# Other tables of order and places, searched on with GpSimd's column operations missing turns

## The chip, the cores and the metric

The kernel runs on one NeuronCore of a Trainium2 chip. The metric is the device time of one execution in microseconds (us), the median of several runs. The core has five engines that run side by side, each through its own queue in the order in which the program issued its work: TensorE (PE, matrix products, with PEld for its weight loads), VectorE (DVE), ScalarE (ACT), GpSimd (POOL) and SyncE (SP, which here only issues DMAs). An instruction that needs another engine's result waits for it, and what is queued behind it on its engine waits with it.

## The reference

The input is x, 2048 rows of 512 float32 values. A layer norm of x goes into two branches, which are multiplied:

```
xn = layernorm(x)
# A: linear attention, 32 heads of 16
q, k, v = split(xn @ wqkv)
pq, pk = phi(q), phi(k)                  # phi(t) = (t + 1 if t > 0 else exp(t)) + 1e-6
o = (pq @ (pk^T v)) / (pq . sum(pk) + 1e-6)
s = o @ wo
# B: a mixer over neighbouring rows, then an MLP
h = gelu(layernorm(xn) @ w1)             # its four quarters are shifted by +1, -1, +2, -2 rows
x1 = xn + shifted(h) @ w2
b = x1 + gelu(layernorm(x1) @ w3) @ w4   # w3: 512 x 1376
out = x + s * silu(b)
```

## The kernel before

The rows lie in 16 tiles of 128 rows, and four tiles make a block. A float32 matrix product is done as three products of rounded parts: each operand is split into a high part (a copy rounded on ScalarE, names that end in `h`) and a low part (what is left, a subtraction on VectorE, names that end in `l`). `products` (line names L133 for all matmuls) issues high x high, high x low and low x high. Many products are also folded by sums of quarters, for which VectorE makes the forms (`xf`, `kq_f`).

The program doesn't issue its work at once. `Plan.add` collects some 5,700 operations in the order of the source, each with its engine and what it reads and writes. They are 3,315 of TensorE, 860 of VectorE, 812 of ScalarE, 216 of GpSimd and 491 of SP. `Plan.emit` then issues them in the order of a written table, `ORDER_OF_ALL`, in which a number n stands for the n-th operation that was added. A second table, `PLACES`, holds the buffer number of each of 1,781 tiles in the pools. So the first table alone sets the order of each engine's queue, and both together set which buffer is reused and when.

GpSimd has three kinds of work. It issues the DMAs that add to what is in the buffer (`gather`, L212). It works on halo columns (two columns of a tile, L538 and L539). And it makes the statistics of the layer norms on columns, 128 partitions by one to four values: `scale_x` makes `w` (L183), `rs` by a power (L451), `ns` (L183) and `nm` (L178) for a block of rows. `spread` makes for a block the two rows of values that the branch B needs:

- `pu` and minus the mean (`an`) on GpSimd, then the power into `an` (L451),
- a transposition of `an` on TensorE into `ab` (L138), a copy to `ar` on ScalarE, and two stores by SP into the rows `arow` and `nrow` in memory,
- from `nrow` GpSimd's gathers add the row to the block's transposed input `xt`, whose parts `u_0h` to `u_3l` and forms `xs_0h` to `xs_3l` are the operands of the products of q and k in that block (`pbx`, `pex`, `pax`).

Blocks are numbered 0 to 3: `ab1` stands first in TensorE's queue, then `ab0`, `ab2` and `ab3`. The profile leaves out such numbers, so all four are `ab` there. `x4` to `x7` are the normalized tiles of block 1, made by ScalarE from `rs` and `nm`.

VectorE's operations are of two kinds for what follows: those with two inputs in SBUF (the subtractions of the low parts, the forms, most of `kr`, `ke` and `qr`) and those that read PSUM (`qi`, `qk`, `kt`) or one input (the `bn_stats` of block 1).

Of the kernel before, what the change touches and what calls it, by code (L numbers as in the profile page):

```python
# [245 lines left out]
def linear_attn_gated_by_mixer(  # L246
# [1336 lines left out]
    for b in LINE:  # L1583
# [11 lines left out]
        0, 15, 16, 4, 12, 20, 1, 11, 17, 2, 14, 23, 32, 18, 44, 19, 13, 53, 21, 22, 97, 35, 45, 26, 46, 98, 47, 174,  # L1595
        123, 48, 29, 24, 96, 33, 175, 25, 105, 49, 38, 102, 124, 99, 103, 51, 41, 34, 108, 106, 125, 100, 176, 54,
        104, 50, 101, 109, 56, 27, 126, 52, 62, 36, 55, 28, 107, 111, 37, 59, 112, 30, 113, 301, 243, 65, 178, 110,
        114, 31, 3, 115, 127, 177, 117, 179, 118, 6, 66, 5, 119, 240, 180, 142, 186, 158, 246, 116, 67, 39, 128,
        120, 42, 143, 68, 237, 181, 129, 203, 69, 204, 43, 121, 182, 159, 40, 205, 474, 187, 130, 160, 206, 207, 70,
        57, 9, 161, 122, 131, 71, 162, 163, 7, 183, 164, 58, 165, 483, 144, 135, 166, 63, 74, 145, 146, 244, 10, 75,  # L1600
        132, 147, 220, 167, 221, 60, 76, 8, 222, 197, 64, 188, 200, 77, 223, 260, 224, 133, 61, 225, 78, 189, 477,
        241, 136, 403, 83, 247, 148, 184, 194, 480, 84, 195, 242, 190, 191, 79, 256, 149, 137, 248, 198, 501, 245,
        85, 238, 226, 150, 80, 86, 284, 72, 285, 268, 168, 286, 134, 208, 239, 138, 192, 169, 209, 193, 88, 210,
        250, 139, 211, 151, 212, 249, 89, 199, 251, 196, 185, 227, 152, 287, 170, 272, 215, 201, 288, 140, 289, 153,
        87, 252, 290, 92, 402, 291, 253, 292, 309, 81, 255, 228, 404, 202, 232, 264, 154, 281, 293, 73, 481, 213,
        302, 278, 214, 155, 305, 275, 229, 296, 257, 279, 303, 294, 337, 93, 280, 156, 269, 331, 311, 230, 304, 273,
        261, 171, 231, 274, 90, 276, 313, 325, 265, 282, 172, 349, 338, 283, 141, 216, 475, 334, 335, 332, 94, 482,
        277, 366, 339, 336, 306, 484, 363, 367, 340, 307, 328, 317, 405, 326, 233, 333, 321, 360, 368, 364, 406,
        314, 365, 476, 407, 341, 369, 342, 322, 1133, 343, 258, 344, 408, 310, 295, 478, 345, 743, 329, 259, 727,
        330, 315, 361, 82, 362, 312, 217, 487, 346, 254, 347, 234, 297, 348, 95, 409, 262, 410, 497, 350, 411, 357,  # L1610
        319, 157, 358, 390, 327, 370, 354, 263, 412, 413, 266, 386, 373, 546, 414, 392, 91, 394, 355, 388, 356, 493,
        359, 393, 415, 416, 505, 395, 396, 417, 423, 267, 424, 270, 418, 419, 479, 316, 430, 420, 389, 425, 485,
        426, 397, 421, 431, 400, 391, 427, 486, 432, 271, 422, 433, 434, 488, 371, 401, 435, 547, 428, 436, 308,
        442, 443, 429, 444, 235, 548, 509, 445, 323, 387, 446, 236, 489, 218, 549, 510, 490, 550, 298, 551, 320,
        492, 447, 398, 553, 219, 318, 554, 555, 491, 437, 511, 556, 399, 733, 557, 173, 378, 558, 449, 438, 450,
        559, 451, 494, 448, 452, 374, 453, 454, 579, 498, 552, 455, 580, 581, 582, 379, 372, 583, 512, 560, 439,
        459, 324, 513, 460, 351, 461, 502, 567, 440, 456, 568, 462, 299, 382, 463, 506, 464, 614, 352, 300, 465,
        584, 615, 381, 380, 611, 441, 469, 561, 724, 562, 617, 526, 470, 563, 569, 620, 522, 457, 564, 565, 570,
        471, 525, 571, 621, 566, 353, 572, 472, 618, 385, 495, 619, 629, 458, 616, 573, 496, 626, 730, 612, 514,
        377, 627, 585, 635, 628, 574, 613, 531, 586, 499, 587, 575, 588, 751, 589, 593, 622, 500, 590, 375, 591,  # L1620
        535, 632, 466, 473, 636, 592, 637, 885, 542, 638, 639, 594, 630, 503, 596, 530, 597, 507, 598, 534, 599,
        576, 536, 631, 747, 600, 532, 538, 601, 577, 796, 540, 640, 703, 376, 623, 602, 624, 642, 533, 641, 625,
        537, 633, 603, 539, 634, 643, 656, 606, 541, 657, 644, 725, 649, 543, 700, 544, 658, 467, 659, 660, 726,
        661, 508, 2057, 645, 646, 662, 595, 504, 650, 709, 518, 701, 607, 647, 710, 383, 675, 578, 521, 676, 648,
        711, 468, 384, 677, 678, 608, 679, 545, 680, 728, 668, 681, 669, 706, 731, 651, 609, 652, 734, 704, 653,
        604, 654, 729, 685, 686, 737, 605, 687, 732, 670, 702, 707, 735, 671, 755, 688, 672, 655, 517, 673, 736,
        797, 674, 689, 738, 690, 705, 691, 803, 712, 804, 663, 759, 805, 739, 760, 708, 664, 740, 718, 519, 713,
        742, 798, 692, 799, 529, 761, 806, 800, 1121, 695, 693, 807, 741, 714, 808, 801, 694, 809, 719, 756, 715,
        1134, 716, 802, 717, 829, 748, 665, 830, 810, 515, 831, 666, 744, 832, 833, 523, 811, 516, 834, 752, 812,
        696, 817, 720, 721, 762, 697, 861, 864, 763, 862, 1135, 698, 813, 610, 764, 814, 863, 520, 873, 682, 722,  # L1630
        818, 887, 819, 820, 683, 821, 822, 723, 870, 823, 988, 871, 865, 772, 767, 872, 835, 867, 684, 868, 1136,
        768, 836, 785, 775, 837, 1153, 524, 874, 757, 1122, 815, 869, 784, 843, 838, 758, 839, 816, 840, 1175, 841,
        781, 866, 780, 824, 876, 1068, 667, 877, 842, 878, 788, 886, 882, 883, 786, 745, 1181, 879, 782, 880, 1154,
        776, 825, 846, 847, 848, 1157, 787, 849, 826, 779, 906, 789, 1158, 899, 1117, 790, 900, 827, 771, 881, 749,
        907, 1201, 875, 746, 884, 908, 783, 527, 909, 1129, 910, 750, 964, 853, 911, 791, 901, 794, 699, 850, 851,
        912, 902, 795, 903, 1159, 904, 792, 965, 844, 966, 1183, 852, 932, 854, 933, 905, 934, 1160, 935, 889, 855,
        936, 856, 888, 937, 845, 1118, 920, 890, 921, 922, 793, 895, 923, 924, 1163, 857, 753, 925, 970, 1184, 971,
        528, 926, 972, 1155, 1002, 896, 913, 891, 914, 967, 754, 858, 1003, 893, 939, 940, 897, 892, 941, 828, 1004,
        859, 915, 894, 1123, 916, 982, 1171, 942, 943, 944, 1141, 976, 1125, 977, 945, 1167, 973, 989, 974, 1143,
        975, 956, 1165, 985, 1067, 949, 777, 917, 918, 978, 968, 1005, 1124, 969, 1006, 986, 957, 1007, 919, 950,  # L1640
        951, 1144, 938, 958, 987, 927, 1009, 860, 1010, 1008, 952, 928, 2162, 953, 1011, 1069, 1012, 1168, 929,
        1023, 1104, 1161, 954, 765, 1016, 1130, 930, 898, 1017, 955, 1013, 778, 1014, 1088, 959, 1177, 1018, 1019,
        1015, 766, 1024, 1178, 1025, 983, 773, 992, 1156, 1020, 984, 960, 769, 1026, 1173, 1070, 1027, 774, 1089,
        961, 1035, 1162, 1036, 770, 1119, 1085, 1179, 979, 946, 962, 980, 981, 1166, 1073, 1021, 990, 1037, 1139,
        1038, 991, 1028, 1169, 1090, 993, 1029, 1039, 1126, 1074, 1086, 1087, 1071, 1097, 947, 1079, 1022, 1042,
        1137, 1120, 1040, 1043, 994, 1230, 1072, 1044, 998, 1045, 1041, 1140, 1298, 1046, 1075, 1047, 1142, 1103,
        1100, 1138, 1048, 1082, 1296, 1083, 1084, 1000, 999, 1101, 1030, 1052, 1053, 995, 1131, 1054, 1098, 1077,
        1094, 1132, 997, 1095, 1096, 2172, 996, 1055, 1076, 1151, 1080, 2056, 1059, 1081, 1078, 1091, 1170, 1049,
        1092, 1056, 1105, 1149, 1127, 1057, 1297, 1031, 1202, 1203, 1058, 1150, 1216, 1050, 1102, 1231, 1147, 1232,
        1107, 1304, 1051, 1217, 1152, 1106, 1204, 948, 1205, 1032, 1145, 1128, 1233, 1206, 1109, 1033, 1099, 1093,  # L1650
        2068, 1234, 1110, 1148, 1062, 1235, 1236, 1146, 1244, 1063, 1112, 1218, 1199, 1245, 1286, 1207, 2069, 1064,
        1219, 1176, 1299, 1305, 1220, 931, 1221, 2066, 1246, 1108, 1237, 1060, 1238, 1113, 1208, 1180, 1321, 1065,
        1306, 1239, 1115, 1174, 1209, 1240, 2059, 1189, 1247, 1114, 1248, 1210, 1172, 1241, 2058, 1116, 1249, 1200,
# [353 lines left out]
```

## Time and profile before

| | us |
|---|---|
| median of three runs | 506.41 (505.35 to 509.16) |
| the profiled execution | 505.57 |
| its span, from the first instruction to the last | 503.9 |
| mean granted TensorE clock over the span | 0.994 of full speed |

The times in the views are counted from the start of the span. A line of the order of time has the start, the duration, engine, source line, operation, what is written and read by the program's names without buffer numbers, the shapes, a count, and in brackets the idle time of the engine just before with what ended it. In the view of waits a line says who waited for whom, the sum in us, the number of waits and the longest.

### The profile page before, as it was taken

How to read it: one execution, taken by the hardware profiler on the slowest of the kernel's cores; microseconds unless marked ns; L12 is line 12 of the kernel's file. 1: busy time of each engine (PE TensorE's matmuls, PEld its weight loads, DVE VectorE, ACT ScalarE, POOL GpSimd, SP SyncE). 2: the span in 40 equal slices, each digit the busy share in tenths (PEclk: the TensorE clock that was granted, in tenths of full speed). 3: DMA queues.
4: the chain of work that ended last, by engine and by line, in shares of the span. 5: the costliest groups of instructions: out<-in, count | busy, mean ns of one | idle time of the engine just before them, and what ended most of it. 6: DMA issues, size and time to landing. Idle time of an engine off the chain costs nothing.

```text
span 503.9 us, 10127 instructions
## 1 busy us (share of the span) xinstructions
PE 491.9 (98%) x3340; PEld 449.4 (89%) x3340; DVE 436.4 (87%) x860; ACT 377.9 (75%) x871; POOL 142.9 (28%) x220
## 2 busy tenths in 40 slices
PE   9999799999999999999999999999999999999996
PEld 5777587888688989898999999999999999999996
DVE  5999696696999989899999999989989889886764
ACT  5999699795876888999899877566688746664531
POOL 1795802555643131331022000000000034443230
PEclk9999899999999999999999999999999999999999
DMA  7959696899898798989779878764779999999998
GB/s 240 317 124 281 132 301 197 177 327 281 219 285 222 181 262 226 234 223 270 245 182 269 289 245 282 229 221 144 211 229 308 300 237 212 277 245 282 271 245 234
DMA packets 90925, 121.60 MB, mean 241 GB/s; under 512 B 10744, under 2 KB 42392, under 8 KB 90872
## 3 DMA queue, kind: packets, MB, share of 16 engines
q1 hardware_dynamic: 78488, 98.93, 60.4%
q0 software_dynamic: 12384, 22.03, 26.1%
q8 instruction: 26, 0.43, 0.4%
q14 instruction: 27, 0.22, 0.1%
HBM read 74.63 MB, written 42.09 MB: 232 GB/s over the span
## 4 chain that ended last, share of the span: by engine, by line
PE 68%; DVE 2%; DMA 2%; ACT 1%; issue 1%; SPq 1%; DVEq 0%; ACTq 0%
PE pbd L133 12%; PE pb L133 11%; PE h L133 8%; PE ped L133 6%; PE pe L133 5%; PE pbs L133 4%; PE pad L133 3%; PE pbm L133 3%; PE pa L133 3%; PE a L133 2%; PE pes L133 2%; PE pem L133 2%; PE g L133 2%; PE pas L133 1%; DMA y_0t<-y_0d 1%; PE pam L133 1%
## 5 line engine op out<-in xcount | busy, mean ns | idle before, releaser
L212 POOL DMA_DIRECT2D xo<-x1d x12 | 10.9, 907 | 147.9 <-DVE xo L178 138.5
L212 POOL DMA_DIRECT2D o<-xnd x16 | 14.2, 908 | 67.2 <-ACT o L155 30.8
L155 ACT ACTIVATE th<-xo 128x512 f32<-128x512 f32 (+1 forms) x16 | 9.9, 617 | 17.5 <-DVE xo L188 9.6
L212 POOL DMA_DIRECT2D zacc<-ke x12 | 10.7, 891 | 38.9 <-DMA zacc<-ke 10.6
L212 POOL DMA_DIRECT2D th<-in_x x14 | 12.5, 945 | 29.8 <-DVE th L188 16.9
L212 POOL DMA_DIRECT2D xt<-nrow x16 | 15.2, 1245 | 1.3 <-DMA nrow<-ar 0.9
L183 POOL TENSOR_SCALAR w<-mv 128x4 f32<-128x4 f32 (+2 forms) x10 | 4.8, 478 | 37.5 <-ACT sq L155 37.2
L155 ACT ACTIVATE y<-o,nm,rs 128x512 f32<-128x512 f32 x16 | 12.3, 807 | 0.0
L155 ACT ACTIVATE ht<-ht 128x512 f32<-128x512 f32 x16 | 9.9, 624 | 2.5 <-DVE ht L178 2.5
L155 ACT ACTIVATE sq<-o,mv 128x512 f32<-128x512 f32 x16 | 11.5, 720 | 0.2
L155 ACT ACTIVATE u<-pb 128x256 f32<-128x256 f32 x20 | 7.6, 381 | 5.3 <-PE pb L133 5.2
L188 DVE SCALAR_TENSOR_TENSOR qz<-pq,zb 128x512 f32<-128x512 f32 x16 | 10.9, 681 | 0.8 <-ACT zb L155 0.6
L178 DVE TENSOR_TENSOR ht<-h,abc 128x512 f32<-128x512 f32 x16 | 10.9, 686 | 0.6 <-PE h L133 0.5
L188 DVE SCALAR_TENSOR_TENSOR pq<-pq,rd 128x512 f32<-128x512 f32 x16 | 10.8, 681 | 0.2
L1278 DVE TENSOR_REDUCE den<-qz 128x32 f32<-128x512 f32 x16 | 10.9, 679 | 0.1
L155 ACT ACTIVATE sq<-o 128x512 f32<-128x512 f32 x16 | 10.0, 628 | 0.6 <-DMA o<-xnd 0.3
L155 ACT ACTIVATE pa<-pb 128x256 f32<-128x256 f32 x20 | 7.3, 368 | 4.0 <-PE pb L133 3.8
L451 POOL TENSOR_TENSOR rs<-w,nhalf 128x4 f32<-128x4 f32 (+2 forms) x10 | 9.8, 982 | 0.8
L155 ACT ACTIVATE p<-pe 128x256 f32<-128x256 f32 x20 | 7.6, 378 | 2.7 <-PE pe L133 2.6
L155 ACT ACTIVATE x<-x,nm,rs 128x512 f32<-128x512 f32 x12 | 9.4, 804 | 0.0
L155 ACT ACTIVATE xo<-pbd 128x256 f32<-128x256 f32 x6 | 2.3, 382 | 9.0 <-PE pbd L133 9.0
L155 ACT ACTIVATE sq<-x,mv 128x512 f32<-128x512 f32 x12 | 8.5, 711 | 0.0
(2018 smaller groups left out, 2526.1 us busy)
## 6 DMA issues: line engine op xcount, KB each, us to landing
w_s<-in_w SPq DMA_DIRECT2D x23, 256.0 KB, 5.1
x<-in_x SPq DMA_DIRECT2D x16, 256.0 KB, 5.1
xt<-in_xt SPq DMA_DIRECT2D x16, 256.0 KB, 5.7
xnd<-x SPq DMA_DIRECT2D x16, 256.0 KB, 4.4
xt<-nrow POOLq DMA_DIRECT2D x16, 256.0 KB, 6.8
pqd<-qr SPq DMA_DIRECT2D x16, 256.0 KB, 3.6
pq<-pqd SPq DMA_DIRECT2D x16, 256.0 KB, 3.9
o<-xnd POOLq DMA_DIRECT2D x16, 256.0 KB, 5.5
```

Of the source, the lines that this page charges most:

```text
L133: lambda: nc.tensor.matmul(out.get(), lhs.get(), rhs.get(), start=start, stop=stop, skip_group_check=more))
L155: nc.scalar.activation(out.get(), src.get(), func, scale=get(scale), **kw)
L178: self.vec(eng, out, [a, b], lambda: self.e(eng).tensor_tensor(out.get(), a.get(), b.get(), op=op), True)
L183: lambda: self.e(eng).tensor_scalar(out.get(), a.get(), get(s1), get(s2), **kw), False,
L188: lambda: self.nc.vector.scalar_tensor_tensor(out.get(), a.get(), get(s), b.get(), op0=op0, op1=op1),
L212: lambda: self.nc.gpsimd.dma_start(out.get(), get(src), accum_op=ALU.add), mb=mb)
L451: lambda: g.tensor_tensor(out.get(), src.get(), nh.get(), op=ALU.pow))
L1278: pl.add("DVE", .6, .68, [t], [den], lambda: nc.vector.tensor_reduce(den.get(), t.get().rearrange("p (h d) -> p h d", d=DH), axis=AX.X, op ...
```

## The change

Both tables are replaced, and nothing else. Every operation, its operands' names, engine and arithmetic stay as they were. In the new tables 398 of the 3,315 TensorE operations have the same rank in TensorE's queue as before; the median shift is 3 ranks and the largest 45. VectorE's median shift is 1 rank (largest 29), ScalarE's 2 (42), GpSimd's 1 (39) and SP's 3 (29). 1,432 of the 1,781 buffer numbers differ. The description of the change says how the new tables were made: by searching on from tables like these with the rule that GpSimd's column operations miss their turns between VectorE's operations.

The diff is two tables of some 370 lines each way. This is its core, the first two lines of the order and the stretch with block 2's `pu` (number 486) and its power (488):

```diff
     ORDER_OF_ALL = (
-        0, 15, 16, 4, 12, 20, 1, 11, 17, 2, 14, 23, 32, 18, 44, 19, 13, 53, 21, 22, 97, 35, 45, 26, 46, 98, 47, 174,
-        123, 48, 29, 24, 96, 33, 175, 25, 105, 49, 38, 102, 124, 99, 103, 51, 41, 34, 108, 106, 125, 100, 176, 54,
...
-        426, 397, 421, 431, 400, 391, 427, 486, 432, 271, 422, 433, 434, 488, 371, 401, 435, 547, 428, 436, 308,
...
+        1, 16, 0, 20, 2, 5, 11, 15, 4, 12, 17, 13, 3, 23, 14, 32, 18, 45, 19, 35, 21, 44, 97, 22, 6, 26, 46, 174,
+        98, 47, 53, 123, 24, 48, 29, 33, 108, 175, 25, 96, 105, 34, 49, 38, 99, 124, 106, 109, 51, 41, 107, 50, 102,
...
+        388, 407, 357, 358, 91, 390, 414, 361, 312, 254, 394, 362, 368, 408, 392, 415, 497, 416, 395, 417, 396, 733,
+        369, 365, 548, 479, 82, 397, 423, 418, 157, 424, 485, 316, 430, 419, 431, 267, 370, 359, 420, 393, 421, 486,
+        270, 432, 373, 389, 433, 422, 425, 271, 488, 426, 434, 400, 387, 427, 428, 401, 435, 429, 442, 443, 320,
...
```

The table below gives, for the operations that the prediction speaks of, how many TensorE operations stand ahead of each in the two orders, as counted in the tables:

| operation | number | engine | before | after |
|---|---|---|---|---|
| power for `ab1` | 251 | GpSimd | 80 | 80 |
| `ab1` | 252 | TensorE | 87 | 90 |
| gathers of `xt` for block 1 | 257, 269, 261, 265 | GpSimd | 100 to 111 | 108 to 118 |
| `ab0` | 405 | TensorE | 123 | 146 |
| last `qi` before the run (`qi3`) | 350 | VectorE | 144 | 143 |
| power of `rs` for block 1 | 367 | GpSimd | 121 | 146 |
| `ns` of block 1 | 368 | GpSimd | 127 | 155 |
| `nm` of block 1 | 369 | GpSimd | 130 | 157 |
| `x4` | 370 | ScalarE | 148 | 165 |
| gather of `kr` (tile 2) | 157 | GpSimd | 146 | 161 |
| `pu` for `ab2` | 486 | GpSimd | 169 | 168 |
| `u_3h` of block 1 | 270 | ScalarE | 160 | 168 |
| first use of that `u_3h` | 426 | TensorE | 165 | 171 |
| power for `ab2` | 488 | GpSimd | 172 | 171 |
| `u_3l` of block 1 | 271 | VectorE | 170 | 171 |
| `ab2` | 489 | TensorE | 181 | 181 |
| next `qi` (`qi4`) | 448 | VectorE | 195 | 192 |

726 rows, old and new, of tables (ORDER_OF_ALL, PLACES) are left out of this document.

## The prediction

> **What bounds the kernel now.** I read the page first, then the busy time of TensorE by stretches, then who TensorE waited for, then the order of time on GpSimd, VectorE, TensorE and ScalarE around the two longest of those waits.
>
> ```profile
> span 503.9 us, 10127 instructions
> ## 1 busy us (share of the span) xinstructions
> PE 491.9 (98%) x3340; PEld 449.4 (89%) x3340; DVE 436.4 (87%) x860; ACT 377.9 (75%) x871; POOL 142.9 (28%) x220
> ```
>
> TensorE is busy for 491.9 of 503.9 us. An order of work changes no matmul, so all that a better order can win is the other 12.0 us, and what a slow clock costs inside the busy time. The stretches with the most idle time in the middle of the run are these two (columns: length, PE busy, granted clock, DMA share, GB/s):
>
> ```profile
> 25.00:37.50 12.50, 11.51 (x51) 1.00 0.58 125
> ...
> 50.00:62.50 12.50, 9.52 (x35) 0.86 0.60 135
> ```
>
> In the second one TensorE lost 3.0 us of busy time, and the clock was granted at 0.86, which is 0.14 x 12.5 = 1.7 us more. The view of waits of TensorE says for whom:
>
> ```profile
> PE ab L138 <- POOL an L451: 4.0, 2, 3.0
> PE pam L133 <- ACT o L155: 1.2, 1, 1.2
> PE warm L133 <- POOL ones L367: 1.0, 1, 1.0
> ```
>
> `ab` is the small transposition in `spread`, of which TensorE needs the result of GpSimd's power `an`. GpSimd in order of time, all operations on 128x4 columns but the gather:
>
> ```profile
> 26.64 2.64 POOL L451 TENSOR_TENSOR an<-pu,nhalf 128x4 f32<-128x4 f32 x1
> ...
> 39.04 2.52 POOL L183 TENSOR_SCALAR ns<-rs 128x4 f32<-128x4 f32 x1
> 41.64 0.20 POOL L178 TENSOR_TENSOR nm<-mv,ns 128x4 f32<-128x4 f32 x1
> 41.92 0.22 POOL L183 TENSOR_SCALAR an<-mv 128x4 f32<-128x4 f32 x1
> 44.13 0.93 POOL L212 DMA_DIRECT2D zacc<-kr  x1 [1.98 <-DVE u_1l L178]
> 48.04 4.90 POOL L183 TENSOR_SCALAR pu<-mv 128x4 f32<-128x4 f32 x1 [2.98 <-ACT sq L155]
> 53.02 1.03 POOL L451 TENSOR_TENSOR an<-pu,nhalf 128x4 f32<-128x4 f32 x1
> ```
>
> The same kind of column operation takes 0.2 us at 41.92, 2.52 at 39.04 and 4.90 at 48.04; the same power takes 1.03 us at 53.02 and 2.64 at 26.64. VectorE shows why:
>
> ```profile
> 41.37 1.61 DVE L188 SCALAR_TENSOR_TENSOR qi<-q,rs,cq 128x512 f32<-128x512 f32 x2
> ...
> 50.66 0.42 DVE L178 TENSOR_TENSOR xf<-xt 128x256 f32<-128x256 f32 x1
> 50.99 0.69 DVE L188 SCALAR_TENSOR_TENSOR qr<-qe,qi 128x512 f32<-128x512 f32 x1
> ...
> 52.20 0.69 DVE L178 TENSOR_TENSOR kq_t30l<-kq_f,kq_t30h 128x512 fp32r<-128x512 f32 x1
> 55.76 0.69 DVE L178 TENSOR_TENSOR xs_2l<-xf,xs_2h 128x512 fp32r<-128x512 f32 x1 [2.87 <-ACT xs_2h L155]
> ```
>
> From 42.90 to 52.8 VectorE runs operations with two inputs in SBUF without a break (0.6 us apart at 512 columns, 0.33 at 256). `pu` ends at 52.94, 0.2 us after the last of them stops. `ns` ends at 41.56, 0.2 us after `qi` starts, which reads PSUM. So a column operation gets its turn when VectorE reads PSUM or stands still, and not between two operations with two SBUF inputs. TensorE and ScalarE pay for it:
>
> ```profile
> 27.95 0.40 PE L133 MATMUL q<-wq_1h,u_1l 128*128 128x512 f32 x1
> 29.33 0.27 PE L138 MATMUL ab<-ident,an 128*8 128x128 f32 x1 [0.99 <-POOL an L451]
> ...
> 50.74 0.40 PE L133 MATMUL pex<-wq_3l,xs_3h 128*128 128x512 f32 x1
> 54.11 0.27 PE L138 MATMUL ab<-ident,an 128*8 128x128 f32 x1 [2.98 <-POOL an L451]
> ...
> 58.10 0.40 PE L133 MATMUL pbx<-kq_t30h,xs_2h 128*128 128x512 f32 x1
> 58.33 0.40 PE L133 MATMUL pbx<-kq_t30l,xs_2h 128*128 128x512 f32 x1
> ```
>
> A matmul of 512 columns starts 0.23 us after the one before. The first transposition (`ab1`) came 1.38 - 0.23 = 1.15 us late, the third (`ab2`) 3.37 - 0.23 = 3.1 us, and with the clock `ab2` cost 4.8 us.
>
> **The change, part by part.** Only the tables differ, so I counted in them how many operations of an engine stand ahead of each.
>
> *ab1.* It stood behind 87 TensorE operations and now stands behind 90: 3 x 0.23 = 0.7 us more cover. Its power now follows a VectorE operation that reads PSUM (`kt`, the 43rd on VectorE); before, it followed the start of three with two SBUF inputs. If the power is as late as before, 1.15 - 0.7 = 0.45 us of wait is left; if it gets its turn, none; were it to miss the turn and start where the three operations behind it end, with TensorE at its 92nd, 2 x 0.23 + 1.03 = 1.5. I take 0.3, between the first two, since the PSUM reader stands there in the table: -0.85 us. What is late next is `nrow` and its gathers, below.
>
> *ab2.* It stands behind 181 TensorE operations in both tables, and `pu` and its power stand 13 and 10 ahead of it, before 12 and 9. That alone gives 0.2 us. What differs is VectorE: the new table has its last PSUM reader (`qi3`) behind 143 TensorE operations, and then 21 operations with two SBUF inputs until `qi4` behind 192; before it was 22, from 147 on. GpSimd has in that run the power of `rs1` for block 1 (behind 146), `ns` (155), `nm` (157), a gather of `kr` (161), `pu` (168) and the power (171). Before, the first three were done before the run began. So the new run holds more column operations. But ScalarE's `x4` now needs `nm` just ahead of `u_3h`:
>
> ```profile
> 42.98 0.80 ACT L155 ACTIVATE x<-x,nm,rs 128x512 f32<-128x512 f32 x1
> ...
> 45.91 0.62 ACT L155 ACTIVATE u_3h<-xt 128x512 fp32r<-128x512 f32 x1
> ...
> 54.42 0.27 ACT L155 ACTIVATE ar<-ab 8x128 f32<-8x128 f32 x1 [2.86 <-PE ab L138]
> ```
>
> If `ns` and `nm` miss their turns, ScalarE stops at `x4`, VectorE runs on to its 80th operation (`u_3l`, which needs `u_3h`, behind 171) and stands still. Then `ns` 0.2, `nm` 0.2, `x4` 0.80 and `u_3h` 0.62 follow one another: 1.8 us, of which 0.1 is covered, since TensorE needs `u_3h` behind 171 operations. TensorE waits 1.7 us, and queued behind that wait are the other products of `pax` and `pex`. In the same standstill (x4 and u_3h, 1.4 us) GpSimd gets through the gather (0.93) and `pu` (0.2), and the power starts; `ab2` has ten matmuls more, 2.3 us, and isn't late. The clock stays up, as it did at the 1.15 us of `ab1`. So 4.8 us go and 1.7 come: -3.1. Bounds: nothing comes (-4.8) or all of it comes back (below, +4.7).
>
> *Gathers of xt for block 1.* They stand behind 108 to 118 TensorE operations instead of 100 to 111, their first users on ScalarE and VectorE behind 135 to 152 instead of 132 to 151. The tightest is `xt1_1`, with 30 operations between, 7.0 us, where it had 36:
>
> ```profile
> xt<-nrow POOLq DMA_DIRECT2D x16, 256.0 KB, 6.8
> ```
>
> 6.8 us of landing leaves 0.2. Bounds: 0 and +1.0 (the move towards its user, 6 x 0.23 = 1.4, less what ab1's shorter wait gives back to its chain); I take +0.4.
>
> *SP's queue and the buffer numbers.* SP's loads and stores move by a median of 3 places, and 1432 of 1781 buffer numbers change. A new buffer can bring a wait for its last user. The one such wait of TensorE is `pam` for ScalarE's `o`, 1.2 us, so I bound these from -1.2 to +1.4 (one more such wait, and a little) and take 0: the loads that SP issues for the turned `y`, which the chain of block 0 hangs on, stand within 13 TensorE operations of where they stood, 3 us at most, to either side. What SP has queued behind a waiting store are loads for later stages.
>
> *The rest of GpSimd's columns (halos, w2, nm2).* No wait of TensorE for GpSimd but `ab` and the first memset stands in the view, so their price is 0 now; what hides them is the tens of matmuls between. Uncovered, each would cost up to the 4.90 of `pu`.
>
> Sum: -0.85 - 3.1 + 0.4 = -3.55. The profiled execution took 505.57 us (span 503.9), which is 0.84 under the median of 506.41. 505.57 - 3.55 = 502.0; half of the 0.84 is added, since runs lie to both sides: **502.4 us**.
>
> **Rivals.**
>
> *All turns are had.* VectorE's 74th and 75th operations wait for ScalarE's `xs_0h` and `xs_1h`, and such a short standstill can let `ns` and `nm` through. Against it: before, the run of 22 had no such hole. Then nothing comes at `u_3h`: 505.57 - 4.8 - 0.85 + 0.4 = 500.3, and 500.7 for the median.
>
> The Trainium skill, in SBUF — State Buffer, section Who interferes with whom, has a rule that gives this time too: of a VectorE instruction with two SBUF inputs and a GpSimd instruction that reads SBUF, the one issued first holds the shared port pair for its whole length, and the other blocks until then. By that rule alone a column operation would lose at most one VectorE operation, 0.6 us, in the old order as in the new. The row of `pu` speaks against that last part: it lost eight in a row.
>
> *The wait moves and keeps its size.* If the power of `rs1` misses `qi3` too, it joins the queue at the standstill: 1.03 + 0.2 + 0.2 + 0.80 + 0.62 = 2.9 us, and the clock falls as it did after 3.1: 1.7 more. 4.6 us come where 4.8 go, and the change doesn't do what it says: 504.9, 505.3 for the median. For it: the power has one PSUM reader only to meet.
>
> *Slower.* If, at that standstill, `pu` isn't through when `u_3h` arrives, it meets VectorE's next run: six operations of 0.6 and two of 0.33 are 4.3 us, then `pu` 0.2 and the power 1.03, 5.5 us against 2.3 of matmuls: 3.2 of wait and 1.7 of clock on top, 509.8, or 510.2. It decides from the point where the gather ahead of `pu` takes more than the 1.4 us of `x4` and `u_3h` less `pu`'s 0.2; the row at 44.13 has 0.93, which speaks against it.
>
> **How the numbers follow.** The forecast 0.42, all turns 0.22, same size elsewhere 0.22, slower 0.14. One per cent, 5.1 us, is about what a measurement of this kernel can tell from no change. Faster by more means under 501.3: 0.65 of the second case and 0.3 of the first, 0.27. Slower by more means over 511.5: not quite half of the last case and a fifth of the third for a wait of the +1.4 kind and more, 0.11. The rest is 0.62. The range 499.3 to 508.0 leaves out most of the slower case and the far end of the best. The likeliest case alone, with the bounds of its terms, runs from 500.7 to 504.5.
>
> **What would show it.** Right: `ab` is gone from TensorE's waits or under 0.5 us, the granted clock is 1.00 from 50 to 62.5, `ns` or `nm` is stretched over several us up to about 48, and TensorE waits about 1.7 us for `u_3h`. Wrong: a clock under 1.00 there, an `ab` that is late by more than 1 us, or a wait of over 1 us for `xf` or `u` of block 1 behind the gathers; and any new wait of TensorE past 62.5 us.

## The result and the profile after

| | before | after |
|---|---|---|
| median | 506.91 us (502.07 to 509.55, 18 runs) | 502.16 us (499.30 to 506.51, 18 runs) |
| ratio of after to before | | 0.9905, 95% [0.9878, 0.9933] |
| the profiled execution | 505.57 us, span 503.9 | 506.51 us, span 504.8 |

The change saves 4.8 us of 506.9 (3.4 to 6.2), 0.95%; the forecast had it at 4.0 of 506.4. The profiled execution of the changed kernel happens to be the longest of its 18 runs; a second profile of it, shown further down, took 501.76 us.

The page of the profile, the span and the busy time of TensorE:

```profile
span 504.8 us, 10113 instructions
...
PE 491.5 (97%) x3340; PEld 448.9 (89%) x3340; DVE 433.7 (86%) x860; ACT 377.7 (75%) x871; POOL 135.5 (27%) x220
```

GpSimd is busy for 135.5 us in the same operations that took 142.9. The column operations of L183, `pu` and `ns` among them, take 12.06 us together where they took 22.40; others take longer, such as the halo copies of L538 with 19.50 instead of 16.21. TensorE's idle time is 504.8 - 491.5 = 13.3 us here, where it was 12.0. To see where it went, the busy time by stretches (length, PE busy, PEld, DVE, ACT and POOL busy, granted clock, DMA share, GB/s):

```profile
25.00:37.50 12.50, 12.50 (x56) 10.00 (x55) 12.25 (x25) 12.13 (x26) 8.22 (x12) 1.00 0.67 168
...
50.00:62.50 12.50, 12.50 (x56) 9.71 (x55) 11.21 (x19) 12.31 (x23) 7.84 (x10) 1.00 0.78 180
...
100.00:112.50 12.50, 9.96 (x44) 7.71 (x43) 9.57 (x19) 9.20 (x17) 9.28 (x11) 1.00 0.90 239
112.50:125.00 12.50, 12.50 (x49) 10.03 (x48) 8.11 (x14) 7.80 (x14) 7.63 (x20) 0.86 0.76 181
```

The two stretches in which TensorE waited for `ab` before (11.51 and 9.52 us busy, the second at a clock of 0.86) are full, at full clock. In this execution the same kind of loss, 2.5 us and a clock of 0.86 behind it, stands 50 us later, and the stretch from 125 to 137.5 us has 2.3 us idle, at full clock, where it had 1.15. TensorE's waits name them:

```profile
PE pbx L133 <- DVE xs_2l L178: 2.5, 1, 2.5
PE warm L133 <- POOL ones L367: 1.2, 1, 1.2
PE g L133 <- ACT k14h L155: 1.2, 1, 1.2
PE pbx L133 <- DVE qk L188: 0.9, 1, 0.9
```

`xs_2l` is the first loss, `k14h` and `qk` make up the second. `ab` is gone from the list. GpSimd in order of time, through the stretch with `ns` and `nm` of block 1 and `pu` of block 2:

```profile
42.90 0.70 POOL L183 TENSOR_SCALAR ns<-rs 128x4 f32<-128x4 f32 x1
43.68 0.22 POOL L178 TENSOR_TENSOR nm<-mv,ns 128x4 f32<-128x4 f32 x1
...
47.39 0.47 POOL L183 TENSOR_SCALAR pu<-mv 128x4 f32<-128x4 f32 x1 [2.27 <-ACT sq L155]
47.94 1.12 POOL L451 TENSOR_TENSOR an<-pu,nhalf 128x4 f32<-128x4 f32 x1
```

`pu` takes 0.47 us where it took 4.90, and `ns`, which was to miss its turns up to about 48 us, takes 0.70. VectorE in the same stretch:

```profile
45.04 0.68 DVE L178 TENSOR_TENSOR xs_0l<-xf,xs_0h 128x512 fp32r<-128x512 f32 x1
45.91 0.69 DVE L178 TENSOR_TENSOR xs_1l<-xf,xs_1h 128x512 fp32r<-128x512 f32 x1 [0.19 <-ACT xs_1h L155]
46.52 0.68 DVE L178 TENSOR_TENSOR kq_t21l<-kq_f,kq_t21h 128x512 fp32r<-128x512 f32 x1
47.12 0.69 DVE L178 TENSOR_TENSOR u_2l<-xt,u_2h 128x512 fp32r<-128x512 f32 x1
```

From 45.04 to 45.91 it is 0.87 us instead of 0.60: VectorE stood some 0.27 us for ScalarE's `xs_1h`. `pu` asks two operations after that, while two-input operations are running, and gets its turn at once. TensorE therefore meets both `u_3h` and the transposition on time, 0.23 us after the matmul before each:

```profile
48.47 0.40 PE L133 MATMUL pax<-wk_2h,u_2l 128*128 128x512 f32 x1
48.70 0.39 PE L133 MATMUL pax<-wk_3h,u_3h 128*128 128x512 f32 x1
...
50.97 0.40 PE L133 MATMUL pex<-wq_3l,xs_3h 128*128 128x512 f32 x1
51.20 0.27 PE L138 MATMUL ab<-ident,an 128*8 128x128 f32 x1
```

The new loss, the 2.5 us for `xs_2l`, is a chain over three engines:

```profile
99.54 3.58 POOL L178 TENSOR_TENSOR hal<-hal,hm 128x64 f32<-128x64 f32 x1 [9.05 <-DMA hm<-nrow]
...
103.79 1.46 POOL L212 DMA_DIRECT2D zacc<-ke  x1
```

```profile
109.67 0.69 DVE L178 TENSOR_TENSOR x11l<-x,x11h 128x512 fp32r<-128x512 f32 x1 [2.81 <-DMA zacc<-ke]
...
110.88 0.68 DVE L178 TENSOR_TENSOR xs_2l<-xf,xs_2h 128x512 fp32r<-128x512 f32 x1
```

`hal`, a GpSimd operation on 128x64 with two inputs, misses six turns. The gather of `ke` behind it in GpSimd's queue starts late, at 103.79 (99.74 in the second profile below), and the buffer of that `ke` is the one into which the new places put `x11l`. So VectorE stands 2.81 us for the gather's end, and `xs_2l`, two operations behind `x11l`, is late for TensorE. In the old places `x11l` had the buffer of `wr_00`, a load.

### The profile page after: what moved, and what is told of

It reads as the page before. It is cut to its first block, busy times and chain, and to the rows that moved or that the text cites. A ratio compares the mean times of both kernels' runs of the same rounds, so it can differ in the third digit from the quotient of the medians.

```text
span 504.8 us, 10113 instructions
## 1 busy us (share of the span) xinstructions
PE 491.5 (97%) x3340; PEld 448.9 (89%) x3340; DVE 433.7 (86%) x860; ACT 377.7 (75%) x871; POOL 135.5 (27%) x220
## 4 chain that ended last, share of the span: by engine, by line
PE 55%; DMA 8%; DVE 5%; issue 2%; ACT 2%; SPq 1%; POOL 0%; DVEq 0%; ACTq 0%; POOLq 0%
PE pb L133 11%; PE pbd L133 10%; PE pe L133 6%; PE ped L133 5%; PE pbs L133 5%; PE pad L133 3%; PE pa L133 3%; PE a L133 2%; PE pes L133 2%; PE h L133 2%; PE pbm L133 2%; DMA th<-in_x 1%; DMA o<-xnd 1%; PE pas L133 1%; PE pem L133 1%
## 5 line engine op out<-in xcount | busy, mean ns | idle before, releaser
L212 POOL DMA_DIRECT2D zacc<-ke x12 | 13.0, 1085 | 23.2 <-DMA zacc<-ke 11.4
L183 POOL TENSOR_SCALAR w<-mv 128x4 f32<-128x4 f32 (+2 forms) x10 | 3.5, 348 | 45.9 <-ACT sq L155 37.4
L188 DVE SCALAR_TENSOR_TENSOR qk<-pbx,ns,p5x 128x512 f32<-128x512 f32 x6 | 4.5, 749 | 4.6 <-PE pbx L133 4.2
```

Source lines behind the costliest of these rows:

```text
L183: lambda: self.e(eng).tensor_scalar(out.get(), a.get(), get(s1), get(s2), **kw), False,
L188: lambda: self.nc.vector.scalar_tensor_tensor(out.get(), a.get(), get(s), b.get(), op0=op0, op1=op1),
L212: lambda: self.nc.gpsimd.dma_start(out.get(), get(src), accum_op=ALU.add), mb=mb)
```

## The experiments

**Both kernels a second time.** No edit.

> The kernel before, unchanged, looked at a second time. Theory A (the order decides who misses its turn): pu at 48 us is stretched to about 4.9 us again, ns at 39 to about 2.5, and TensorE waits about 3 us for ab2. Theory B (each execution draws its turns by chance): the stretched column operations are others, or pu passes in well under 2 us and the wait for ab2 is much smaller.

> The changed kernel, unchanged, looked at a second time. Theory A (order): GpSimd's hal at 99.5 us is stretched to about 3.6 us again, and TensorE waits about 2.7 us for xs_2l at 108.7. Theory B (chance): hal takes under 1.5 us, VectorE doesn't stand still ahead of x11l, the wait at 108.7 is gone and the execution is 3 to 5 us shorter than the first one profiled (506.5).

`before_again` took 511.22 us. `pu` in its order of time:

```profile
47.31 4.89 POOL L183 TENSOR_SCALAR pu<-mv 128x4 f32<-128x4 f32 x1 [3.65 <-ACT sq L155]
```

It asked 0.7 us earlier in the span than in the first profile and took 4.89 us (4.90 there); `ns` took 2.50 (2.52). These stretches are no chance of one execution. (That this execution is 5 us longer comes from elsewhere: waits of 1.9 and 2.5 us for `o` between 204 and 210 us, with a low clock behind them.) `after_again` took 501.76 us. Its page, two lines of its waits, and GpSimd around `hal`:

```profile
span 500.1 us, 10113 instructions
...
PE 489.5 (98%) x3340; PEld 447.8 (90%) x3340; DVE 433.7 (87%) x860; ACT 377.2 (75%) x871; POOL 133.5 (27%) x220
```

```profile
PE pbx L133 <- DVE qk L188: 1.3, 1, 1.3
...
PE k L133 <- ACT u_1h L155: 1.0, 1, 1.0
```

```profile
98.02 0.83 POOL L178 TENSOR_TENSOR hal<-hal,hm 128x64 f32<-128x64 f32 x1 [8.00 <-DMA hm<-nrow]
...
99.74 1.45 POOL L212 DMA_DIRECT2D zacc<-ke  x1
```

Here `hal` asked earlier in VectorE's run, got its turn, and the 2.5 us for `xs_2l` did not come: Theory B's signs, for this operation. By these two profiles it depends on when the transfer of `hm`, for which `hal` waits, lands in VectorE's run.

**One cause alone, in the kernel before: VectorE stands when `pu` asks.** VectorE's `xs_3l` (401) and the `xs_3h` on ScalarE that it waits for (400) are put ahead in the old order, so that VectorE has a hole there, which means that it stands still for a moment. The second kernel, `after_x11l`, is the changed one with the buffers of `x11l` and `wt_00h` exchanged.

```diff
 # before_stand: ORDER_OF_ALL
-        426, 397, 421, 431, 400, 391, 427, 486, 432, 271, 422, 433, 434, 488, 371, 401, 435,
+        426, 397, 400, 401, 421, 431, 391, 427, 486, 432, 271, 422, 433, 434, 488, 371, 435,
 # after_x11l: PLACES (x11l, wt_00h)
-        41, 1, 39, 34, 1, 10, 45,
+        41, 1, 39, 54, 1, 10, 45,
...
-        24, 14, 36, 54, 80, 1, 1,
+        24, 14, 36, 34, 80, 1, 1,
```

> The kernel before with one VectorE operation (xs_3l) and the ScalarE operation that it needs (xs_3h) put two places ahead, so that VectorE stands still for about 0.5 us just when pu asks at 48.0 us. If a column operation gets through when VectorE stands still, pu takes under 1 us, ab2 is no longer late, TensorE's clock stays at 1.00 from 50 to 62.5 us and the time falls by about 4.3 us (4.8 less 0.5). If pu's delay has another cause than VectorE's run, nothing changes.

`before_stand`: 502.54 us, ratio 0.995 [0.9914, 0.9987], some 2.5 us (0.7 to 4.4), where 4.3 were expected. VectorE and GpSimd:

```profile
47.68 0.69 DVE L178 TENSOR_TENSOR xs_3l<-xf,xs_3h 128x512 fp32r<-128x512 f32 x1 [0.51 <-ACT xs_3h L155]
```

```profile
47.22 0.19 POOL L183 TENSOR_SCALAR pu<-mv 128x4 f32<-128x4 f32 x1 [2.99 <-ACT sq L155]
47.49 1.04 POOL L451 TENSOR_TENSOR an<-pu,nhalf 128x4 f32<-128x4 f32 x1
48.61 0.75 POOL L183 TENSOR_SCALAR w<-mv 128x4 f32<-128x4 f32 x1
...
50.86 0.68 POOL L183 TENSOR_SCALAR ns<-rs 128x4 f32<-128x4 f32 x1
```

Half a microsecond of standstill let `pu` through and took away the wait for `ab` and the low clock; TensorE waits 0.7 us for `u_3l` in its place. In this profile `ab1` isn't late either: its power took 1.05 us where it had taken 2.64, though nothing ahead of it was moved, so that wait is one that some executions of the old order do without. But `w` and `ns`, behind the hole, got their turns too, between two operations with two SBUF inputs, where `pu` had missed eight. So such a boundary is not shut in itself.

> The changed kernel with the buffers of x11l and wt_00h exchanged, so that VectorE's x11l no longer waits for the gather of ke8 (ScalarE's wt_00h does in its place). If the buffer is the cause of the wait at 108.7 us, VectorE doesn't stand still ahead of x11l and TensorE doesn't wait there, whatever hal takes; the profiled execution is then some 4 us shorter than the first one of the changed kernel (506.5). Against the kernel before about 0.985 to 0.99. If the gather was late for all and the buffer only one of several, the wait stays and goes to another operation.

`after_x11l`: 500.9 us, 0.9914 [0.9876, 0.9951]. In its profile `hal` had its turn anyway (0.40 us), so it does not tell what the exchanged buffer is worth. Inconclusive. It has a wait of 1.5 us for `qk` and a low clock right behind it, to which the last section comes back.

**Does a late wait have to stand at that boundary?** One kernel was to give the old order a late wait ahead of `pu`, the other to take away the wait of the new order ahead of `xf` by a buffer exchange.

```diff
 # before_self: ORDER_OF_ALL, a half of xf moved up
-        400, 391, 427, 486, ... 445, 323, 387, 446,
+        400, 391, 387, 427, 486, ... 445, 323, 446,
 # after_nolate: PLACES (qe of tile 2, xf_3)
-        2, 89, 78, 79, 37, ... 10, 62, 14, 19, 28,
+        2, 89, 78, 19, 37, ... 10, 62, 14, 79, 28,
```

> The kernel before with one VectorE operation (the second half of xf_2, 128x256) put four places ahead, directly behind the first half, whose result it adds to. It then has to wait for the operation just before it, some 0.12 us, at the end of the operation during which pu asks. Theory L (a column operation gets its turn where VectorE's next operation has a wait that ends late): pu takes under 0.6 us in place of 4.9, ab2 is no longer late, the clock stays at 1.00 from 50 to 62.5 us, and the ratio to the kernel before is about 0.992 (4.3 us). Theory S (only a read of PSUM or a standstill of about half a microsecond lets it in): pu still takes over 4 us and the ratio is 1.00.

> The changed kernel with the buffers of xf_3 and qe (tile 2) exchanged: xf_3, ahead of which pu got its turn at 47.7 us, no longer waits for a matmul that ends just then. Theory L: pu misses that turn; if it misses the following ones too, up to the next late wait, it takes 1 to 5 us and TensorE waits 0 to 3 us for ab2 again. If the turn had another cause, pu takes about 0.5 us as before and nothing changes.

`before_self` took 506.67 us, 0.9977 [0.9932, 1.0022], and its `pu` 4.89. Its premise was wrong: the two halves of `xf` are different columns, so no late wait arose, and the run says only that moving a half alone does nothing. `after_nolate` took 501.42 us, 0.9882 [0.9828, 0.9936]: with the wait ahead of `xf` gone, `pu` still took 0.47 us. Theory L fell. What the kernels with a short `pu` share is a hole in VectorE's run, either just as `pu` asks (`before_stand`) or a few operations earlier.

**The wait for `qk` at 130 us.** In `after_again` VectorE stands for the load of `wr_11`, whose buffer is another in the new places, and TensorE then waits for `qk`:

```profile
124.59 0.42 DVE L188 SCALAR_TENSOR_TENSOR wt<-wt,wr 128x256 f32<-128x256 f32 x1 [3.55 <-DMA wr<-in_w]
```

```profile
129.47 0.50 PE L133 MATMUL pbx<-kq_t40h,u_2h 128*128 128x512 f32 x1 [1.26 <-DVE qk L188]
```

```diff
 # after_wr11: the exchange of after_x11l, the load of wr_11 (989) four places up in SP's queue, its buffer exchanged with u_0h's
-        957, 927, 1069, ... 1141, 989, 1023,
+        957, 927, 989, 1069, ... 1141, 1023,
-        36, 34, 76, 14, 33, ... 1, 1, 26, 66, 87,
+        36, 34, 76, 66, 33, ... 1, 1, 26, 14, 87,
```

> The changed kernel with x11l's buffer exchanged as in the run before and, further, wr_11 in the buffer that u_0h had (free at 112.2 us, where wt_00's is free only at 116.2), with its load 4 places ahead in SP's queue. VectorE stood still from 121.0 to 124.6 us for that load, and TensorE then waited 1.4 to 1.7 us for qk. If the new buffer is the cause, VectorE's standstill there is under 1 us, the wait for qk falls to about 0.5 us, and the time is about 1 us under the changed kernel's (501.2 us, ratio to the kernel before 0.988). If other loads are late as well, the standstill moves and the time is the same as the changed kernel's.

The standstill is gone (that operation starts at 120.97) and so is the wait for `qk`. The time is 502.79 us, 0.99 [0.9843, 0.9956], not to be told from the changed kernel's: its profile has 1.8 us of wait for `u_1h` at the start in its place. That the late load makes `qk` late is shown, for its buffer and its place in SP's queue together; a gain in the total is not.

**Both parts of the change in the old order, beside the change.** `before_both` is `before_stand` with `ab1` (252), its copy (253) and store (255) behind five more matmuls. `before_pulate` makes `pu` ask later in the unbroken run, by moving ScalarE's `sq` (485), which `pu` waits for, behind `xs_3h` (400).

```diff
 # before_both: the edit of before_stand, and
-        87, 252, 290, 92, 402, 291, 253, 292, 309, 81, 255, 228, 404, 202, 232,
+        87, 290, 92, 402, 291, 292, 309, 81, 228, 404, 202, 252, 253, 255, 232,
 # before_pulate
-        389, 425, 485, 426, 397, 421, 431, 400, 391,
+        389, 425, 426, 397, 421, 431, 400, 485, 391,
```

> The kernel before with two small edits: VectorE's xs_3l with ScalarE's xs_3h two places ahead (the standstill of before_stand), and ab1 with its copy and its store behind five more matmuls in TensorE's queue, so that ab1 is needed 1.15 us later. Theory A (the two waits for ab are the change's whole gain): TensorE waits for ab less than 0.3 us in all, and the ratio to the kernel before is that of the changed kernel in the same session within 0.003, about 0.991. Theory B (the other 5,600 moved operations bring a good part themselves): it stays at 0.994 or above while the changed kernel is at 0.990.

> The changed kernel, unchanged, timed beside before_both: 0.9905 of the kernel before as it was in its first timing, within 0.003. Its profile, a third look: pu takes under 0.6 us again, and hal and the wait at 108 us depend on when hm lands.

> The kernel before with ScalarE's sq (tile 11) and xs_3h exchanged, so that pu asks 0.6 us later, at about 48.6 us, in the same run of VectorE. Theory P (whether a turn is had depends on when the operation asks): pu passes at one of the next two boundaries, under 1.3 us, and ab2 is on time. Theory R (in this run no boundary lets a column operation in): pu misses all boundaries that are left, takes about 4.3 us and ends at the same time as before, 52.9, and TensorE's wait for ab2 stays at 3 us.

`before_both` took 502.99 us, 0.9909 [0.9873, 0.9945]; the change on the same chip 501.01, 0.9883 [0.9837, 0.9929]. So two small edits around `ab1` and `ab2`, with all buffers as before, give the change's gain within what can be measured, 4.6 us of 507 (2.8 to 6.4) against 5.9 (3.6 to 8.3); what all the other shifts and the new buffers bring can't be told from nothing here. `after_five`, the third profile of the changed kernel, has `pu` at 0.47 us again, `hal` at 0.44 and no wait for `xs_2l`. Waits of `before_both`, with no `ab` among them:

```profile
PE pbx L133 <- DVE qk L188: 2.3, 1, 2.3
PE pam L133 <- ACT o L155: 1.7, 1, 1.7
...
PE pax L133 <- DVE u_3l L178: 0.7, 1, 0.7
```

In `before_pulate` (505.45 us) `pu` asked at 48.76 and took 4.07 us, to the end of VectorE's run again, as Theory R has it:

```profile
48.76 4.07 POOL L183 TENSOR_SCALAR pu<-mv 128x4 f32<-128x4 f32 x1 [4.01 <-ACT sq L155]
```

**Turns by themselves.** The computation is left out in this kernel. VectorE runs stretches of 26 subtractions of 128x512 with two SBUF inputs, 0.602 us apart, each begun by a wait for ScalarE. In stretch k of the first sixteen a column operation of GpSimd asks when subtraction k (from 0) is done, so in the one that follows; in the last nine, subtraction 13 has a late wait for the one before it (0.71 us instead of 0.602), and k runs from 12 to 20.

```diff
+    for late, asks in ((None, range(0, 16)), (13, range(12, 21))):
+        for k in asks:
+            nc.scalar.activation(h[:, :], xs[0][:, :], AF.Identity, bias=c[:, 0:1], scale=1.0)
+            for i in range(26):
+                a = h if i == 0 else d[i - 1] if i == late else xs[i % 16]
+                b = xs[(i + 5) % 16] if i else last
+                nc.vector.tensor_tensor(d[i][:, :], a[:, :], b[:, :], op=ALU.subtract)
+                if i == k:
+                    nc.gpsimd.tensor_scalar(c[:, :], d[k][:, 0:4], 0.5, 0.25, op0=ALU.mult, op1=ALU.add)
+            last = d[25]
```

> A measurement by itself: the kernel's computation is left out, and what it writes is not the reference's. VectorE runs 25 stretches of 26 subtractions with two inputs in SBUF (128x512, none waiting for another engine), and between two stretches it has to wait for its own last result and for ScalarE. In each stretch GpSimd has one column operation (128x4) that needs the result of VectorE's k-th subtraction, k = 0 to 15 in the first 16 stretches, so that it asks during subtraction k+1. In the last 9 stretches subtraction 13 has to wait for the result of subtraction 12, and k is 12 to 20. Theory Q (a column operation gets its turn at the next boundary in the first half dozen operations after VectorE's last late wait, and none later): it takes under 0.8 us for k up to 4 to 6, and from there on lasts to the end of its stretch, (24 - k) x 0.6 us, 10 us for k = 8; in the last 9 stretches it takes under 0.8 us for k = 12 to 18 or so and lasts to the end for the later ones. Theory S (only a standstill or a read of PSUM lets it in): it lasts to the end of its stretch for every k of the first 16, 14 us for k = 1. Theory C (chance): short and long ones in no order of k.

GpSimd in order of time, for k = 4 and 5 and, behind the late wait, for k = 17, 18 and 19:

```profile
75.21 0.50 POOL L42 TENSOR_SCALAR c<-d 128x4 f32<-128x4 f32 x1 [15.95 <-DVE d L40]
91.66 11.94 POOL L42 TENSOR_SCALAR c<-d 128x4 f32<-128x4 f32 x1 [15.95 <-DVE d L40]
...
361.67 0.50 POOL L42 TENSOR_SCALAR c<-d 128x4 f32<-128x4 f32 x1 [16.43 <-DVE d L40]
378.24 4.11 POOL L42 TENSOR_SCALAR c<-d 128x4 f32<-128x4 f32 x1 [16.06 <-DVE d L40]
395.54 3.51 POOL L42 TENSOR_SCALAR c<-d 128x4 f32<-128x4 f32 x1 [13.19 <-DVE d L40]
```

Asked in the sixth operation (k = 4), it gets the next boundary, and so it does for every smaller k (0.49 to 0.62 us). Asked in the seventh (k = 5), it misses all 19 that are left, 11.94 us, and for every larger k it lasts to the end of the stretch too. The late wait in mid-stretch starts the count anew: six more, then none (k = 17 is the sixth from it, k = 18 the seventh). This is Theory Q's rule: in this kernel, what counts is how many operations VectorE has run since it last stood.

It fits the three operations of the real kernel on which the waits above hang. Counted in VectorE's order of time, `pu` of before asked in the 13th operation since VectorE's last hole and `ns` in the 7th, and both missed every turn. In the changed kernel `ns` asked in the 6th, `pu` in the 3rd, and both got theirs. `hal` asked in the 7th in the first profile and in the 5th in `after_again`.

**What starts the count again.** Some column operations of the two orders and their variants asked in the seventh operation or later and still got their turn: `nm` in the 7th in all six profiles of the new order, right behind `ns` (43.68 above), and `ns` in the 7th in `before_stand` (50.86 above) and `before_both`, behind a `w` that had got its own. So the same kernel again, with two column operations in seven stretches (the first with k = 3, the second with k = 5, 7, 8, 9, 10, 11, 13), and in nine more one column operation near a 13th subtraction that reads PSUM.

```diff
+    for reader, asks in ((None, ((3, 5), (3, 7), (3, 8), ...)), (12, ((10,), (11,), (12,), ...))):
...
+                a = h if i == 0 else z if i == reader else xs[i % 16]
```

> The computation is left out: 16 stretches of 26 VectorE subtractions of 128x512, each begun by a late wait. In the first seven a first column operation of GpSimd asks in the 5th operation and a second one in the 7th, 9th, 10th, 11th, 12th, 13th or 15th. In the other nine the 13th operation reads PSUM, and one column operation asks in the 12th to 17th, 18th, 19th or 20th. Theory N: only a late wait of VectorE starts the count of six. Then the first ones take 0.50 us, all second ones miss every boundary and take 11.3 us for the 7th down to 6.5 for the 15th; and those of the other nine take 0.5 to 0.6 us if asked in the 12th (the PSUM reader is next) and the 13th, and from 7.7 to 4.1 us after it, to the end of the stretch. Theory S: a turn that is had starts the count again, and so does a PSUM reader. Then the second ones asked in the 7th to 11th take 0.50 us, and the later ones, from the 12th on, 8.3 us or less to the end; and those behind the PSUM reader take 0.50 us up to the 18th and 4.1 to 3.5 in the 19th and 20th. A mix of the two (one restarts it, the other doesn't) would show as one group of each.

GpSimd for the pair (3, 7), the second of the pair (3, 8), and for k = 10, 11 and 12 around the PSUM reader:

```profile
27.48 0.50 POOL L47 TENSOR_SCALAR c<-d 128x4 f32<-128x4 f32 x1 [14.38 <-DVE d L45]
29.89 0.50 POOL L47 TENSOR_SCALAR c<-d 128x4 f32<-128x4 f32 x1 [1.91 <-DVE d L45]
...
46.34 10.13 POOL L47 TENSOR_SCALAR c<-d 128x4 f32<-128x4 f32 x1 [2.51 <-DVE d L45]
...
130.47 0.50 POOL L47 TENSOR_SCALAR c<-d 128x4 f32<-128x4 f32 x1 [7.66 <-DVE d L45]
146.91 0.19 POOL L47 TENSOR_SCALAR c<-d 128x4 f32<-128x4 f32 x1 [15.95 <-DVE d L45]
163.36 7.72 POOL L47 TENSOR_SCALAR c<-d 128x4 f32<-128x4 f32 x1 [16.25 <-DVE d L45]
```

Neither theory came out whole. A turn that is had between two-input operations makes the window longer, though not by another six: the second column operation passes when it asks in the 9th operation and misses all from the 10th on. (In the first stretch VectorE still waited for loads, so it says nothing.) A PSUM reader gives a turn as it begins or while it runs, and nothing after: asked in the next operation, 7.72 us.

## Why the prediction came out as it did

The forecast was 502.4 us and the median is 502.16. Of the main steps one was wrong, and that the total fits is in good part luck: other waits of about the same size stood in for it.

*`ab1`: right.* 0.3 us of wait was to be left; none is, and its power had its turn (1.09 us). *`ab2`: right in what goes, not in the way.* Its 4.8 us of wait and clock are gone, but `pu` was to get through in a standstill at `u_3h`, which did not come. `before_both`, which takes away these two waits alone, gains as much as the change within what can be measured.

*The wait for `u_3h`, +1.7: wrong.* The step that failed is the rule read out of the old trace, that a column operation "gets its turn when VectorE reads PSUM or stands still, and not between two operations with two SBUF inputs". The old trace had shown such boundaries only late in a run. Shortly behind a hole they are open (`turns_alone`: up to the sixth operation). `ns` and `nm` met an open one, `x4` and `u_3h` were on time, and `pu` got through behind the short standstill for `xs_1h`, which the first rival had named for `ns` and `nm`. In this stretch that rival, all turns had, is what happened, though the 500.7 us that it gave lies farther from the median than the forecast. The Trainium skill, SBUF — State Buffer, section Who interferes with whom, has an exclusive lock by which the side that issues first blocks the other for its whole instruction; the 0.50 us rows agree with it, and the 11.94 us over 19 instructions does not.

*Gathers of `xt` for block 1, +0.4: none came.* No wait for them stands in the list.

*Buffers and the other shifts, 0 between -1.2 and +1.4: mis-sized.* Idle time of TensorE before was 12.0 us; less the 4.0 of `ab` it would be 8.0. It is 500.1 - 489.5 = 10.6 in `after_again`, so 2.6 us of idle came elsewhere: 1.3 for `qk` (0.7 before) and 1.0 for `u_1h` at the start are the largest that are new. They are not the new tables' alone. `u_1h` is as late in profiles of the old order (1.0 in `before_stand`, 1.2 in `before_pulate`), and `before_both`, with the old buffers and no wait for `ab`, has 502.7 - 491.7 = 11.0 us of idle, 2.3 of it for `qk`. So part of this is what differs from execution to execution, and part may be that TensorE, once `ab` no longer holds it up, comes earlier to operands that are not ready; how much is which was not measured. Why `u_1h` is late at the start stays open. In the first profile `xs_2l` takes the place of much of it, with 2.5 us and the clock on top; the prediction had named a new wait past 62.5 us as a sign against it, and that sign came. Without the 1.7 and the 0.4 the forecast would have been 500.3; with the 2.6 us of other idle, from that one execution, it is 502.9, against the measured 502.16. So the total came out close because two wrong terms, 2.1 us too much and 2.6 too little, nearly cancel. That they do is luck.

*Details of the working.* The stretch with `ab1`, 0.99 us idle, was not among the two with the most idle time: the old trace has 1.15 from 125 to 137.5 us and 1.22 from 200 to 212.5. The clock was to stay up through a wait of 1.7 us, by the 1.15 us of `ab1`; in `after_x11l` a wait of 1.5 us cost it (last section), so that was not safe. And the bounds of the likeliest case, 500.7 to 504.5, do not quite come out of its terms: with `ab1` at 0 or 0.45 us, the gathers at 0 or 1.0 and the buffers at -1.2 or 1.4 they are 500.5 and 504.6. Nothing hangs on it.

*Slower, and the wait that keeps its size: did not come.* They needed GpSimd's queue to stay shut until the standstill at `u_3h`, and it was open.

## What to carry to other kernels

Before an order is built around "GpSimd misses its turns", find what opens them: here a hole of 0.3 to 0.5 us in VectorE's run, within the six operations ahead of the one in which the column operation asks, let `pu` through, and a wait of 3 us and 1.7 us of slow clock went with it (2.5 us of the whole, 0.7 to 4.4, when it was all that was changed). Two edits around the waits that the trace shows did as much, within what can be measured, as a search over the whole order, and a new set of buffers should be read for whom each new reuse makes wait (here `x11l` for a gather, `wt` for a load).

## What the hardware showed unexpectedly

- A 128x4 operation of GpSimd asked in the sixth two-input operation of VectorE since its last hole took 0.50 us, in the seventh 11.94. The count seems to go by operations and not by time: in the changed kernel `hal` missed, asked 2.9 us behind a hole in the 7th operation (some of them of 256 columns), and `ns` passed, asked 2.9 us behind one in the 6th. But `hal` is also the larger operation, so this pair alone doesn't settle it. What in VectorE counts to six no run shows.
- Not all of the real kernel follows it: `nm` with two inputs, at 214 to 223 us, missed one turn (0.71 us) when asked in the 4th or 6th operation. In all six profiles of the old order `nm` at 87 to 92 us took 1.73 us though asked in the first operation behind a hole of about 2 us; GpSimd's gathers of `xt` run beside it, so missed turns need not be the whole of it. And `hal` in `before_both` asked in the 10th operation, two behind one that reads PSUM, and still had the next boundary (0.44 us). These stay open. `w` at 38 us passes in the changed kernel far from any hole of 0.1 us or more; a delay of 0.03 us three operations ahead of it would explain it, if so little counts, which was not tried.
- A wait of the same length doesn't always cost the clock. `ab` came 2.98 us late in the profile of before, with 0.86 granted in its stretch, and 2.98 us late in `before_pulate`, with 1.00:

```profile
50.00:62.50 12.50, 9.52 (x43) 7.41 (x42) 9.04 (x16) 9.69 (x18) 11.16 (x13) 1.00 0.58 136
```

```profile
54.01 0.27 PE L138 MATMUL ab<-ident,an 128*8 128x128 f32 x1 [2.98 <-POOL an L451]
```

The same idle time, 9.52 us of busy, holds 43 matmuls here and 35 there. A much shorter wait can cost it too. `after_x11l` has one of 1.5 us, and 0.86 in its stretch:

```profile
PE pbx L133 <- DVE qk L188: 1.5, 1, 1.5
```

```profile
125.00:137.50 12.50, 10.79 (x39) 8.08 (x38) 11.73 (x22) 8.37 (x16) 8.89 (x20) 0.86 0.93 250
```

The 2.5 us for `xs_2l` in the changed kernel and the 2.3 for `qk` in `before_both` cost it as well, and the 1.7 for `o` in `before_both` and 1.6 in `before_pulate` did not. So between 1.5 and 3 us of wait it can go either way here, and the 1.7 us of clock in the forecast is a price that is paid on some occasions and not on others.
